# Decode attention on one core: engines without a closing barrier, PV of block 0 inside the PE loop, K of two blocks loaded first, and the last rows stored by two queues

## The chip, the cores and the metric

The kernel runs on one core of one Trainium2 chip. The metric is the device time of one execution in microseconds (us). Each DMA leaves 16 completion records in a trace (1776 for the 111 DMAs of the kernel before), and I count it landed at the last of them. A ratio is the mean time of one kernel's fast runs over that of the other kernel's fast runs of the same rounds, so it is not quite the ratio of the medians that stand beside it.

## The reference

```
q: [8, 16, 16, 256]   k, v: [8, 16, 2048, 256]   (bf16)
scores = einsum('bhqd,bhkd->bhqk', q, k) * 256 ** -0.5
attn   = softmax(scores, axis=-1)
out    = einsum('bhqk,bhkd->bhqd', attn, v)
```

There are 128 heads with 16 queries each. K and V are 134 MB each and every byte is used for 16 queries only, so the kernel is a way to stream 268 MB through the core.

## The kernel before

The profile names five engines: PE for the matrix products, DVE (here transposes, maxima and scaling), ACT (here exponentials, scaling and stores), POOL (nearly idle here) and SP (here the loads). `PEld` are PE's weight loads, and `SPq` or `ACTq` marks what the profile gives to an engine's sequencer, such as issuing a DMA. QK is the product that gives the scores, PV the one with V.

The heads are worked on in G = 16 blocks of 8. A block has two units (e = 0, 1) of 4 heads; a unit's K is 4 MB, and so is its V. `KN` holds two units of K and `VB` two units of V, so each load waits until its buffer is free: K until DVE has transposed the old K (`kt`), V of block g until PE has multiplied with V of block g-1 (`pv`).

For each block: DVE transposes K (8 instructions of 2.28 us), PE computes the scores (`qk`, 64 matmuls and 32 weight loads), DVE takes the maximum, ACT the exponential, DVE transposes the probabilities, PE multiplies with V (`pv`, 64 matmuls and 64 weight loads), ACT and DVE scale the result, and ACT stores it.

Every engine has its own list of jobs with semaphores between them. SP's list is the loads, in this order:

```python
        for u in (0, 1):
            k_load(u)                 # K of block 0, each unit in two halves
        v_load(0)
        k_load(2)                     # K of block 1, unit 0
        v_load(1)
        k_load(3)                     # K of block 1, unit 1, in two halves
        for g in range(2, G):
            for u in (2 * g, 2 * g + 1):
                k_load(u)
            for u in (2 * g - 2, 2 * g - 1):
                v_load(u)
        v_load(NU - 2)
        v_load(NU - 1)                # the last unit in pieces of 16 16 8 8 8 4 4 tiles
```

PE's list, of which the steady part is a loop (`nc.Fori`), so that its instructions stand in the program once:

```python
        qk_block(0)
        qk(1, 0, 0)
        qk(1, 0, 1)
        pv(0, 0)                      # PV of block 0 between the pieces of QK of block 1
        qk(1, 1, 0)
        qk(1, 1, 1)
        pv(0, 1)
        qk_block(2)
        for g in range(3, last):
            pv(g - 2, 0)
            pv(g - 2, 1)
            qk_block(g)
        # ... (cut: QK of the last block, PV of the last two)

        def emit_pe(eng):
            jobs = order["pe"]
            head, turns = jobs[:14], [jobs[14 + 6 * x:20 + 6 * x] for x in range(G - 4)]
            emit_jobs(eng, head)
            # ... (cut: checks that all turns wait alike)
            with nc.Fori(0, STEP * len(turns), STEP, ...) as it:
                # ... (cut: one turn, waiting for values that grow by STEP)
            emit_jobs(eng, jobs[14 + 6 * len(turns):])
```

The streams stand in a `Block`, which joins all engines in a barrier at its end. ACT stores the last rows and waits for them.

Of the kernel before, what the change touches and what calls it, by code (L numbers as in the profile page):

```python
# [12 lines left out]
HT = 32  # L13
# [12 lines left out]
def bass_standalone__softmax_full_bidir__sampling_kernel(  # L26
# [10 lines left out]
    G = NH // 8  # L37
    NU = 2 * G
    last = G - 1
# [4 lines left out]
    ku = k.rearrange("b h s d -> (b h s) d").rearrange("(u p t) d -> u p t d", p=128, t=NT)  # L44
# [3 lines left out]
    with ExitStack() as es:  # L48
        ec = es.enter_context
        KN = ec(nc.sbuf_tensor("KN", [128, 2, NT, D], BF16))  # L50
# [8 lines left out]
        O_fin = ec(nc.sbuf_tensor("O_fin", [128, 4, D], BF16))  # L59
# [11 lines left out]
        sem_kn = [ec(nc.semaphore("s_kn%d" % i)) for i in range(2)]  # L71
# [6 lines left out]
        def J(eng, cls, emit, deps=(), dma=None, inc=1):  # L78
            deps = [d for d in deps if d is not None]
            if dma is not None:  # L80
                jb = _Job(eng, cls, emit, deps, dma[0], dma[1], 16)
            else:
                if (eng, cls) not in counters:
                    counters[(eng, cls)] = [ec(nc.semaphore("c_%s_%s" % (eng, cls))), 0]
                c = counters[(eng, cls)]
                c[1] += inc
                jb = _Job(eng, cls, emit, deps, c[0], c[1], inc)
            order[eng].append(jb)
            return jb

        block = ec(nc.Block())

        QR = VB[:, 1, 0:SQ, :].rearrange("p s d -> p (s d)")
        KNf = KN[:].bitcast(F32)
        KBf = KB[:].bitcast(F32)
# [83 lines left out]
                ins = eng.matmul(O_ps[:, bank, 0:D], PT[:, t, :], buf[:, t, :], start=(t == 0), stop=(t == NT - 1))  # L179
            return ins  # L180

        def emit_store(eng, g, e=None):
            dst = out.rearrange("b h s d -> (b h s) d")[g * 128:(g + 1) * 128, :].rearrange("(e r) d -> e r d", e=2)
            if e is None:
                return eng.dma_start(dst.rearrange("e r d -> r e d"), O_fin[:, g % 2, :])
            return eng.dma_start(dst[e], O_fin[e:128:2, 2 + e, :])


        j_idz = J("pool", "prep", lambda eng: eng.memset(ident[:], 0.0))
# [9 lines left out]
        j_qwb, j_qt, j_exp, j_pt, j_px, j_max, j_rab = {}, {}, {}, {}, {}, {}, {}  # L199
        j_ea, j_eb, j_st = {}, {}, {}  # L200

        vparts = {NU - 2: [32, 32], NU - 4: [32, 32], NU - 1: [16, 16, 8, 8, 8, 4, 4]}

        def v_parts(u):
            return vparts.get(u, [HT, HT] if u % 2 else [NT])

        def k_load(u):

            g, e = u // 2, u % 2
            deps = [("kt", g - 1, e, 3)] if g else []  # L210
            if u in (0, 1, 3):
                for h in range(2):
                    j_k[u, h] = J("sp", "ld", lambda eng, h=h, n=HT: eng.dma_start(  # L213
                        KN[:, e, HT * h:HT * h + HT, :], ku[u, :, HT * h:HT * h + HT, :]), deps,
                        dma=(ec(nc.semaphore("s_k%d%d" % (u, h))), 16))
            else:
                n0 = len([x for x in range(e, u, 2) if x not in (0, 1, 3)])
                j_k[u, 0] = j_k[u, 1] = J("sp", "ld", lambda eng, n=NT: eng.dma_start(KN[:, e], ku[u]),
                                          deps, dma=(sem_kn[e], 16 * (n0 + 1)))

        def v_buf(u):

# [2 lines left out]
        def v_load(u):  # L225
            g, e = u // 2, u % 2
            j_v[u] = []
            a = 0
            for x, n in enumerate(v_parts(u)):
                deps = [("kt", g, e, 3)] if g == last else [("pv", g - 1, 1)] if g else [("qt", 0)] if e else []  # L230
                sem = (ec(nc.semaphore("s_vt%d_%d" % (u, x))), 16) if g >= last - 1 else (sem_v[e + x], 16 * (g + 1))
                j_v[u].append(J("sp", "ld", lambda eng, a=a, n=n: eng.dma_start(  # L232
                    v_buf(u)[:, a:a + n, :], vu[u, :, a:a + n, :]), deps, dma=sem))
                a += n


        for u in (0, 1):
            k_load(u)
        v_load(0)
        k_load(2)  # L240
        v_load(1)
        k_load(3)
        for g in range(2, G):
            for u in (2 * g, 2 * g + 1):
                k_load(u)
            for u in (2 * g - 2, 2 * g - 1):
                v_load(u)
        v_load(NU - 2)
        v_load(NU - 1)

# [11 lines left out]
        def qk(g, e, h):  # L262
            j_qk[g, e, h] = J("pe", "qk", lambda eng: emit_qk(eng, e, h),
                              [("kt", g, e, 2 * h + 1), ("qwb", g, e) if h == 0 else None,
                               ("exp", g - 1, h) if g and e == 0 else None])
# [7 lines left out]
        def pv(g, h):  # L273
            j_pv[g, h] = J("pe", "pv", lambda eng: emit_pv(eng, h),
                           [("px", g, h), ("eb", g - 1) if g and h == 0 else None]
                           + (j_v[2 * g] + j_v[2 * g + 1][:1] if h == 0 else j_v[2 * g + 1][1:]))
# [52 lines left out]
        def finish(e):  # L329

            j_eb[last, e] = J("dve", "eb", lambda eng: eng.tensor_scalar(  # L331
                out=O_fin[:, 2 + e, :], in0=O_ps[:, (2 * last + e + 1) % 4, 0:D], scalar1=rab[:, last, e:e + 1],
                scalar2=None, op0=ALU.mult), [("pv", last, 1, e), ("rab", last)])

        def finish_store(e):
            j_st[last, e] = J("act", "st", lambda eng: emit_store(eng, last, e), [("eb", last, e)],
                              dma=(ec(nc.semaphore("s_fin%d" % e)), 16))


        def qk_block(g):  # L340
            for e in range(2):
                for h in range(2):
                    qk(g, e, h)

        qk_block(0)
        qk(1, 0, 0)
        qk(1, 0, 1)
        pv(0, 0)
        qk(1, 1, 0)
        qk(1, 1, 1)  # L350
        pv(0, 1)
        qk_block(2)
        for g in range(3, last):
            pv(g - 2, 0)
            pv(g - 2, 1)
            qk_block(g)
# [19 lines left out]
            softmax_act(g)  # L376
        evac_a(last - 1)
        store(last - 1)
        finish_store(0)
        finish_store(1)  # L380

        j_qt[0] = J("dve", "qt", emit_qt, j_q)
        for g in range(G):
# [16 lines left out]
        px(last, 1)  # L400
        finish(0)
        finish(1)

        tables = {"kt": j_kt, "qwb": j_qwb, "qt": j_qt, "qk": j_qk, "exp": j_exp, "pt": j_pt, "px": j_px, "max": j_max,
                  "rab": j_rab, "ea": j_ea, "eb": j_eb, "st": j_st, "pv": j_pv}
# [12 lines left out]
        def emit_jobs(eng, jobs):  # L418
            known = {}
            for jb in jobs:  # L420
                for sem, val in needs(jb).values():
                    if known.get(id(sem), 0) < val:
                        eng.wait_ge(sem, val)
                        known[id(sem)] = val
                jb.emit(eng).then_inc(jb.sem, jb.inc)

        def emit_stream(eng, name):
            emit_jobs(eng, order[name])
            if name == "act":
                for key in (last - 2, last - 1, (last, 0), (last, 1)):  # L430
                    eng.wait_ge(j_st[key].sem, j_st[key].val)

        def emit_pe(eng):

            jobs = order["pe"]
            head, turns = jobs[:14], [jobs[14 + 6 * x:20 + 6 * x] for x in range(G - 4)]
            emit_jobs(eng, head)
            first = [needs(jb) for jb in turns[min(1, len(turns) - 1)]]
            base = 2 + min(1, len(turns) - 1)
            for x, turn in enumerate(turns):  # L440
                for n0, jb in zip(first, turn):
                    n1 = needs(jb)
                    assert all(key in n0 and n0[key][1] + STEP * (x + 2 - base) == val for key, (_, val) in n1.items())
            with nc.Fori(0, STEP * len(turns), STEP, engines=OrderedEngineSet([eng.engine]), head_slot={eng.engine: 0}) as it:
                offs = sorted({val - STEP * (base - 2) for n0 in first for _, val in n0.values()})
                at = {o: eng.snap(it + o) for o in offs}
                for jb, n0 in zip(turns[0], first):
                    for sem, val in n0.values():
                        eng.wait_ge(sem, at[val - STEP * (base - 2)])
                    jb.emit(eng).then_inc(jb.sem, jb.inc)  # L450
            emit_jobs(eng, jobs[14 + 6 * len(turns):])

        @block.sync
        def _(eng):
            emit_stream(eng, "sp")

        @block.tensor
        def _(eng):
            emit_pe(eng)

        @block.scalar
        def _(eng):
            emit_stream(eng, "act")

        @block.vector
        def _(eng):
            emit_stream(eng, "dve")

        @block.gpsimd
        def _(eng):  # L470
            emit_stream(eng, "pool")

# [1 line left out]
_INS = ['q', 'k', 'v']  # L474
_OUTS = [((8, 16, 16, 256), 'bfloat16')]
# [23 lines left out]
```

## Time and profile before

The median was 641.17 us.

| what | before |
|---|---|
| span | 639.5 us |
| bytes moved, mean rate over the span | 270.67 MB, 423 GB/s |
| first K load issued, last V load landed | 2.56 us, 636.05 us |
| landing to landing of 4 MB loads | 9.71 us (432 GB/s) |
| PE, DVE, ACT busy | 77%, 67%, 15% |

The page of the profile shows the 16 DMA engines busy from the first slice to the last (tenths of 40 slices of 16 us, and what they moved in each); among the DMA queues, q1 carries the loads, and q8 instruction packets, of 16 KB each (five, 0.08 MB; I take them for fetches of PE's program; the first came at 63.09 us):

```profile
DMA  9999999999999999999999999999999999999996
GB/s 319 436 427 427 438 419 440 428 427 434 426 434 426 430 441 424 443 426 429 428 426 437 428 430 437 421 446 416 441 428 426 435 424 437 435 427 435 421 422 253
...
q1 hardware_dynamic: 13152, 269.49, 98.7%
...
q8 instruction: 5, 0.08, 0.1%
...
DMA 72%; DVE 23%; PE 3%; issue 1%; SPq 0%; ACT 0%; DVEq 0%; ACTq 0%
```

The reader is to see that the loads are the bound: the chain that ended last is 72% DMA, and where it says DVE, a transpose only frees the buffer for a load that is queued behind others. So the rest of the work costs time only where it lets the load queue run dry.

The last V piece lands at 636.05 us, and the timeline (start, duration, engine, line, what) goes on:

```profile
636.75 0.48 DVE L331 TENSOR_SCALAR O_fin<-O_ps,rab 128x256 bf16<-128x256 f32 x1 [6.64 <-PE O_ps L179]
637.27 0.50 ACTq L186 DMA_DIRECT2D out_dram<-O_fin  x1
```

The store lands at 639.06 us, and a branch, a drain and the barrier of the block take until 639.55.

### The profile page before, as it was taken

To read this page: it belongs to the slowest core of one execution; us is meant where nothing else is said; L and a number is where in the kernel's file an instruction comes from. 1 tells how busy PE (TensorE), PEld (TensorE's weight loads), DVE (VectorE), ACT (ScalarE), POOL (GpSimd) and SP (SyncE) were. 2 spreads that over 40 slices of the span, in tenths; PEclk is the share of its full clock that TensorE was granted. 3 is DMA by queue.
4 is the path that set the end of the run, shared out by engine and by line. 5 is a ranking of instruction groups with operands and counts; after the bars stand their busy time and mean duration, and the time that the engine had idled before them with its cause. 6 is when DMAs were issued, how large, how long until landed. Compare 5 with 4: busy or idle time off the path is not lost.

```text
span 639.5 us, 4835 instructions
## 1 busy us (share of the span) xinstructions
PE 491.4 (77%) x2176; PEld 166.7 (26%) x1680; DVE 428.2 (67%) x372; ACT 99.1 (15%) x208; POOL 4.2 (1%) x7
## 2 busy tenths in 40 slices
PE   0827979876896768958688686797866878686998
PEld 0102313213131221412213132131311313122286
DVE  4866598693857938488483875939569395694861
ACT  2121203030120301202012120211203012030010
POOL 2000000000000000000000000000000000000000
PEclk9977989899897998979899798998989989799899
DMA  9999999999999999999999999999999999999996
GB/s 319 436 427 427 438 419 440 428 427 434 426 434 426 430 441 424 443 426 429 428 426 437 428 430 437 421 446 416 441 428 426 435 424 437 435 427 435 421 422 253
DMA packets 15483, 270.67 MB, mean 423 GB/s; under 512 B 1776, under 2 KB 3824, under 8 KB 4464
## 3 DMA queue, kind: packets, MB, share of 16 engines
q1 hardware_dynamic: 13152, 269.49, 98.7%
q10 hardware_dynamic: 2320, 1.05, 0.6%
q8 instruction: 5, 0.08, 0.1%
q14 instruction: 6, 0.05, 0.0%
HBM read 269.48 MB, written 1.05 MB: 423 GB/s over the span
## 4 chain that ended last, share of the span: by engine, by line
DMA 72%; DVE 23%; PE 3%; issue 1%; SPq 0%; ACT 0%; DVEq 0%; ACTq 0%
DMA KN<-in_k_dram 68%; DVE KB L128 22%; DMA KN<-in_v_dram 5%; PE O_ps L179 2%; PE S_ps L145 1%; PE S_ps L133 1%; DVE PC L159 0%; SPq L112 0%; DVE negm L150 0%; ACT QW L121 0%; DVE O_fin L331 0%; SPq L213 0%; SPq L232 0%; ACT P_sb L154 0%; DVE rab L300 0%
## 5 line engine op out<-in xcount | busy, mean ns | idle before, releaser
L128 DVE STREAM_TRANSPOSE KB<-KN 128x2048 f32<-128x2048 f32 x128 | 284.8, 2281 | 154.3 <-DMA KN<-in_k_dram 131.6
L145 PE MATMUL S_ps<-KB,QW 128*128 128x512 bf16 x528 | 215.9, 418 | 127.4 <-DVE KB L128 127.4
L173 PE MATMUL O_ps<-VB,PT 128*128 128x512 bf16 x896 | 198.9, 383 | 17.7 <-DMA VB<-in_v_dram 17.7
L133 PE MATMUL S_ps<-KB,QW 128*128 128x512 bf16 x496 | 207.1, 417 | 0.0
L145 PEld LDWEIGHTS S_ps<-KB,QW 128*128 128x128 bf16 x528 | 54.4, 103 | 333.8 <-issue 232.4
L173 PEld LDWEIGHTS O_ps<-VB,PT 128*128 128x128 bf16 x896 | 87.5, 99 | 131.8 <-issue 31.1
L121 ACT ACTIVATE QW<-QT 32x128 bf16<-32x128 bf16 x128 | 53.9, 421 | 334.4 <-PE S_ps L133 326.5
L165 DVE COPY PT<-PC 32x1024 bf16<-32x1024 bf16 x128 | 53.3, 416 | 4.3 <-PE O_ps L179 2.6
L159 DVE STREAM_TRANSPOSE PC<-P_sb 128x1024 bf16<-128x1024 bf16 x32 | 37.9, 1224 | 21.1 <-ACT P_sb L154 21.1
L150 DVE TENSOR_REDUCE negm<-S_ps 128x1 f32<-128x2048 f32 x16 | 36.7, 2292 | 7.9 <-PE S_ps L133 7.5
L154 ACT ACTIVATE P_sb<-S_ps,negm 128x1024 bf16<-128x1024 f32 x32 | 35.4, 1110 | 36.1 <-DVE negm L150 26.4
L316 ACT ACTIVATE O_tmp<-O_ps,rab 128x256 f32<-128x256 f32 x15 | 7.1, 474 | 144.2 <-PE O_ps L173 143.4
L179 PE MATMUL O_ps<-KN,PT 128*128 128x256 bf16 x128 | 14.4, 273 | 0.2 <-DMA KN<-in_v_dram 0.2
L179 PE MATMUL O_ps<-VB,PT 128*128 128x256 bf16 x128 | 14.1, 273 | 0.1
L179 PEld LDWEIGHTS O_ps<-VB,PT 128*128 128x128 bf16 x128 | 12.4, 98 | 2.0 <-DVE PT L165 0.6
L179 PEld LDWEIGHTS O_ps<-KN,PT 128*128 128x128 bf16 x128 | 12.3, 98 | 2.2 <-issue 0.5
L331 DVE TENSOR_SCALAR O_fin<-O_ps,rab 128x256 bf16<-128x256 f32 x2 | 1.0, 484 | 11.8 <-PE O_ps L179 11.8
L321 DVE SCALAR_TENSOR_TENSOR O_fin<-O_ps,rab,O_tmp 128x256 bf16<-128x256 f32 x15 | 6.7, 448 | 1.8 <-issue 1.8
L154 ACT ACTIVATION_READ_ACCUMULATOR P_sb<-S_ps,negm 128x1 f32 x32 | 6.3, 196 | 0.0
L115 DVE STREAM_TRANSPOSE QT<-VB 128x2048 f32<-128x2048 f32 x1 | 2.3, 2311 | 5.6 <-DMA VB<-in_q_dram 5.6
L300 DVE TENSOR_SCALAR rab<-mask,rinv 128x2 f32<-128x2 f32 x16 | 3.7, 229 | 0.6
L191 POOL MEMSET PT<- 128x4096 f32 x1 | 3.5, 3512 | 0.0
(11 smaller groups left out, 7.8 us busy)
## 6 DMA issues: line engine op xcount, KB each, us to landing
KN<-in_k_dram SPq DMA_DIRECT2D x29, 4096.0 KB, 29.8
VB<-in_v_dram SPq DMA_DIRECT2D x32, 2048.0 KB, 25.2
VB<-in_v_dram SPq DMA_DIRECT2D x14, 4096.0 KB, 20.0
KN<-in_k_dram SPq DMA_DIRECT2D x6, 2048.0 KB, 21.0
KN<-in_v_dram SPq DMA_DIRECT2D x2, 2048.0 KB, 27.7
KN<-in_v_dram SPq DMA_DIRECT2D x2, 1024.0 KB, 23.4
KN<-in_v_dram SPq DMA_DIRECT2D x3, 512.0 KB, 26.1
VB<-in_q_dram SPq DMA_DIRECT2D x4, 256.0 KB, 4.5
```

The source lines that it names most:

```text
L121: ins = eng.activation(ap_of(dv, dv.offset + 32 * a + e, [[256, 4], [128, 2], [2, 16]]), ap_of(sv, sv.offset + 2 * (2 * g + e), [[64, 4], ...
L128: return eng.transpose(KBf[:, c % R_KB].rearrange("p t i -> p (t i)"), KNf[:, e].rearrange("p t i -> p (t i)")[:, n * c:n * c + n])
L133: return eng.add_instruction(mybir.InstMatmult(start_tensor_calc=start, stop_tensor_calc=stop, ldweights=False, tile_size=(128, 128), tile ...
L145: ins = mm(S_ps[:, 2 * h + c, :], QW[:, e, bp, :], rhs, start=(e == 0 and bp == 0), stop=(e == 1 and bp == 7))
L150: return eng.tensor_reduce(out=negm[:, g:g + 1], in_=S_ps[:].rearrange("p c n -> p (c n)"), axis=AX.X, op=ALU.max, negate=True)
L154: return eng.activation(P_sb[:, 1024 * h:1024 * h + 1024], S_ps[:, 2 * h:2 * h + 2, :].rearrange("p c n -> p (c n)"), ACTF.Exp, bias=negm[ ...
L159: return eng.transpose(PC[:, h].rearrange("p t x -> p (t x)"), P_sb[:, 1024 * h:1024 * h + 1024])
L165: ins = eng.tensor_copy(PT[pr, 32 * h:32 * h + 32, pr], PC[pr, h])
L173: ins = eng.matmul(O_ps[:, 0, :], PT[:, t, :], rhs, start=(t == 0), stop=(t == NT - 1))
L179: ins = eng.matmul(O_ps[:, bank, 0:D], PT[:, t, :], buf[:, t, :], start=(t == 0), stop=(t == NT - 1))
L316: j_ea[g] = J("act", "ea", lambda eng: eng.activation(O_tmp[:], src, ACTF.Copy, scale=rab[:, g, 0:1]), [("pv", g, 1) if g < last - 1 else ...
L321: j_eb[g] = J("dve", "eb", lambda eng: eng.scalar_tensor_tensor(out=O_fin[:, g % 2, :], in0=src, scalar=rab[:, g, 1:2], in1=O_tmp[:], op0= ...
```

## The change

The intent: end each engine by itself, so that no barrier follows the last store; shorten PE's program by taking PV of block 0 into the loop, which then runs 13 turns and not 12; load K of blocks 0 and 1 before any V, in halves, so that QK of block 1 can be done before that PV; and halve the last store over two queues.

```diff
-        block = ec(nc.Block())
...
-        vparts = {..., NU - 1: [16, 16, 8, 8, 8, 4, 4]}
+        vparts = {..., NU - 1: [16, 16, 8, 8, 8, 4, 2, 2]}
...
-            if u in (0, 1, 3):
+            if g < 2:
                 for h in range(2):        # two halves; each now waits for its own half's transpose
...
-        for u in (0, 1):
-            k_load(u)
-        v_load(0)
-        k_load(2)
-        v_load(1)
-        k_load(3)
-        for g in range(2, G):
+        for g in range(G):
             for u in (2 * g, 2 * g + 1):
                 k_load(u)
-            for u in (2 * g - 2, 2 * g - 1):
-                v_load(u)
+            if g:
+                for u in (2 * g - 2, 2 * g - 1):
+                    v_load(u)
...
         qk_block(0)
-        qk(1, 0, 0)
-        qk(1, 0, 1)
-        pv(0, 0)
-        qk(1, 1, 0)
-        qk(1, 1, 1)
-        pv(0, 1)
-        qk_block(2)
-        for g in range(3, last):
+        qk_block(1)
+        for g in range(2, last):
             pv(g - 2, 0)
             pv(g - 2, 1)
             qk_block(g)
...
-        finish_store(0)
-        finish_store(1)
+        finish_store("act", 0, 0, 64)
...
+        finish_store("sp", 1, 0, 32)
+        finish_store("act", 1, 32, 64)
...
-            head, turns = jobs[:14], [jobs[14 + 6 * x:20 + 6 * x] for x in range(G - 4)]
+            head, turns = jobs[:8], [jobs[8 + 6 * x:14 + 6 * x] for x in range(G - 3)]
...
-        @block.sync
-        def _(eng):
-            emit_stream(eng, "sp")
...
+        emit_stream(nc.sync, "sp")
+        emit_stream(nc.scalar, "act")
+        emit_stream(nc.vector, "dve")
+        emit_stream(nc.gpsimd, "pool")
+        emit_pe(nc.tensor)
```

More of the change, by code (lines that the diff above doesn't have):

```diff
@@ L180, in emit_pv1, with emit_store @@
             return ins
-        def emit_store(eng, g, e=None):
+        def emit_store(eng, g, e=None, r0=0, r1=64):
             dst = out.rearrange("b h s d -> (b h s) d")[g * 128:(g + 1) * 128, :].rearrange("(e r) d -> e r d", e=2)
@@ L185, in emit_store @@
                 return eng.dma_start(dst.rearrange("e r d -> r e d"), O_fin[:, g % 2, :])
-            return eng.dma_start(dst[e], O_fin[e:128:2, 2 + e, :])
+            return eng.dma_start(dst[e, r0:r1], O_fin[2 * r0 + e:2 * r1:2, 2 + e, :])
         j_idz = J("pool", "prep", lambda eng: eng.memset(ident[:], 0.0))
@@ L200, in bass_standalone__softmax_full_bidir__sampling_kernel @@
         j_ea, j_eb, j_st = {}, {}, {}
-        vparts = {NU - 2: [32, 32], NU - 4: [32, 32], NU - 1: [16, 16, 8, 8, 8, 4, 4]}
+        vparts = {NU - 2: [32, 32], NU - 4: [32, 32], NU - 1: [16, 16, 8, 8, 8, 4, 2, 2]}
         def v_parts(u):
@@ L209, in k_load @@
             g, e = u // 2, u % 2
-            deps = [("kt", g - 1, e, 3)] if g else []
-            if u in (0, 1, 3):
+            if g < 2:
                 for h in range(2):
                     j_k[u, h] = J("sp", "ld", lambda eng, h=h, n=HT: eng.dma_start(
-                        KN[:, e, HT * h:HT * h + HT, :], ku[u, :, HT * h:HT * h + HT, :]), deps,
-                        dma=(ec(nc.semaphore("s_k%d%d" % (u, h))), 16))
+                        KN[:, e, HT * h:HT * h + HT, :], ku[u, :, HT * h:HT * h + HT, :]),
+                        [("kt", g - 1, e, 2 * h + 1)] if g else [], dma=(ec(nc.semaphore("s_k%d%d" % (u, h))), 16))
             else:
-                n0 = len([x for x in range(e, u, 2) if x not in (0, 1, 3)])
                 j_k[u, 0] = j_k[u, 1] = J("sp", "ld", lambda eng, n=NT: eng.dma_start(KN[:, e], ku[u]),
-                                          deps, dma=(sem_kn[e], 16 * (n0 + 1)))
+                                          [("kt", g - 1, e, 3)], dma=(sem_kn[e], 16 * (g - 1)))
         def v_buf(u):
@@ L333, in finish, with finish_store @@
                 scalar2=None, op0=ALU.mult), [("pv", last, 1, e), ("rab", last)])
-        def finish_store(e):
-            j_st[last, e] = J("act", "st", lambda eng: emit_store(eng, last, e), [("eb", last, e)],
-                              dma=(ec(nc.semaphore("s_fin%d" % e)), 16))
+        def finish_store(eng, e, r0, r1):
+            j_st[last, e, r0] = J(eng, "st", lambda eng: emit_store(eng, last, e, r0, r1),
+                                  [("eb", last, e)],
+                                  dma=(ec(nc.semaphore("s_fin%d_%d" % (e, r0))), 16))
         def qk_block(g):
@@ L428, in emit_stream @@
             emit_jobs(eng, order[name])
-            if name == "act":
-                for key in (last - 2, last - 1, (last, 0), (last, 1)):
-                    eng.wait_ge(j_st[key].sem, j_st[key].val)
+            for key in {"act": (last - 2, last - 1, (last, 0, 0), (last, 1, 32)), "sp": ((last, 1, 0),)}.get(name, ()):
+                eng.wait_ge(j_st[key].sem, j_st[key].val)
         def emit_pe(eng):
             jobs = order["pe"]
-            head, turns = jobs[:14], [jobs[14 + 6 * x:20 + 6 * x] for x in range(G - 4)]
+            head, turns = jobs[:8], [jobs[8 + 6 * x:14 + 6 * x] for x in range(G - 3)]
             emit_jobs(eng, head)
@@ L450, in emit_pe @@
                     jb.emit(eng).then_inc(jb.sem, jb.inc)
-            emit_jobs(eng, jobs[14 + 6 * len(turns):])
-        @block.sync
-        def _(eng):
-            emit_stream(eng, "sp")
-        @block.tensor
-        def _(eng):
-            emit_pe(eng)
-        @block.scalar
-        def _(eng):
-            emit_stream(eng, "act")
-        @block.vector
-        def _(eng):
-            emit_stream(eng, "dve")
-        @block.gpsimd
-        def _(eng):
-            emit_stream(eng, "pool")
+            emit_jobs(eng, jobs[8 + 6 * len(turns):])
+        emit_stream(nc.sync, "sp")
[3 more added lines that the diff above has]
+        emit_pe(nc.tensor)
 _INS = ['q', 'k', 'v']
```

## The prediction

> What bounds the kernel now: the K and V loads. The page's DMA row is 9 tenths in every slice but the last, 423 GB/s over the 639.5 us span; the chain of waits is 72% DMA. By the records of the SP queue's loads, 4 MB land every 9.71 us and the queue never runs dry, from the first K issue at 2.56 us to the last V landing at 636.05 us. Work moved in the middle can't show unless it starves that queue. What can: the head, the tail, disturbances of the stream.

> The tail before (timeline): last V lands 636.05; its 4 PV matmuls end 636.75; DVE's scaling ends 637.24; ACT issues the last store 637.27, landing 639.06; the barrier that closes the block runs from 639.1 to 639.55.

> What the change does:
> 1. No closing barrier, no branches: after the store's wait come 0.47 us of branch, drain and barrier, all critical. Saved: about 0.4 us.
> 2. Last V piece 2 tiles, not 4: two matmuls fewer after the landing, 2 x 0.108 = 0.2 us; one more DMA with shorter packets (a 2 KB packet took 84 ns, an eighth of a 16 KB one 77) costs about 0.1. Net 0.1.
> 3. Last store in halves on SP and ACT: issue to landing was 1.79 us, mostly latency: [...] Half the rows save perhaps 0.15 us.
> 4. K of blocks 0 and 1 first, in halves, then V0: the queue keeps a load ahead (K2's halves can go out at about 17 and 22 us, while K1 lands until 27; K3's at 28 and 32). No gain, no hole: at most +0.1 us.
> 5. PV of block 0 inside the loop: PE has slack (77% busy). PV(0) now ends at about 80 us by my estimate, so V of block 1 is issued some 5 us before the queue would drain. But the PE program gets shorter by some 220 instructions (96 of a QK block, 128 of a PV). [...] This trace shows five 16 KB instruction packets, 1.0 to 1.1 us each (63, 106, 576, 612, 625 us); the load landing after the first came 1.40 us late, never recovered; an 8 KB fetch at 486 us cost 0.98 us more. At the end DMA engines finish over about 3 us (DMA share 0.69 in 632 to 634 us), and the latest sets the last landing. 220 instructions are 14 KB: one PE fetch should go, likely an early one. Gain 0 to 1.4 us, depending on which DMA engine the others hit; I take 0.5; a loss of 0.5 is possible.

> Sum: 0.4 + 0.1 + 0.15 + 0.5, less 0.05: 1.1 us. Predicted 640.1 us, range 639.0 to 640.9. Faster by over 2% (under 628.3): 1%; within 2%: 98%; slower by over 2%: 1%.

> What would show it: nothing after the last store's waits; DVE's last scaling starting about 0.5 us after the last landing, not 0.7; the store's halves landing about 1.65 us after issue; four 16 KB instruction packets; the lateness at 67 us gone or moved; landings still 9.71 us apart.

> What would make it wrong: a hole in the load queue around 50 to 90 us; fetches falling on one DMA engine; the measured time, 1.7 us longer than the span, may hold a closing cost that grows when engines end apart.

"Mostly latency" in point 3 rests on the trace of before: the store's packets took 0.25 us (638.43 to 638.68) of the 1.79. The 0.15 us is my estimate; half of those 0.25 would be 0.13. The 14 KB of point 5 are 220 instructions of 64 bytes, a size that was not shown then; k_pool_stream, below, shows it for POOL (128 memsets to a packet of 8 KB).

## More of the kernel before

The granted clock is the share of PE's full clock that it was allowed.

The timeline between 60 and 93 us (start, duration, engine, line, what) shows PV of block 0 in its two halves, and SP issuing V of block 1 when the second is done; the table of stretches gives from and to in us, the length, the busy time of PE, its weight loads, DVE, ACT and POOL with instruction counts, the granted clock, the share of the DMA engines and GB/s:

```profile
60.70 7.07 PE L173 MATMUL O_ps<-VB,PT 128*128 128x512 bf16 x32
75.59 7.07 PE L173 MATMUL O_ps<-VB,PT 128*128 128x512 bf16 x32
82.69 1.28 SPq L232 DMA_DIRECT2D VB<-in_v_dram  x3
```

```profile
84.00:86.00 2.00, 0.00 (x0) 0.00 (x0) 2.00 (x2) 0.00 (x0) 0.00 (x0) 1.00 0.93 360
86.00:88.00 2.00, 1.26 (x4) 0.34 (x3) 2.00 (x2) 0.00 (x0) 0.00 (x0) 0.79 0.97 410
```

V of block 1 is issued at 82.69 us. The load ahead of it, K of block 2, lands at 86.97 us, 4.3 us later.

## The result, and the profile after

The changed kernel is slower: 646.05 us median (644.84 to 646.44, 6 runs), where the kernel before takes 641.19 us (640.97 to 641.36, 6 runs). The ratio is 1.0072 with a 95% interval of 1.0059 to 1.0085. That is within 2%, as forecast, but on the other side, and 5 us above the upper end of the range. The profiled run took 645.01 us with a span of 643.7 us. Its page, the lines that answer to those shown of before:

```profile
DMA  9999979999999999999999999999999999999996
GB/s 324 425 433 430 438 299 430 448 416 438 426 432 444 414 443 423 431 440 429 435 419 436 436 428 436 420 438 427 435 440 413 443 422 436 436 431 431 417 425 257
...
q1 hardware_dynamic: 13488, 269.51, 98.1%
...
q8 instruction: 5, 0.08, 0.1%
...
DMA 65%; DVE 23%; PE 10%; issue 1%; SPq 1%; ACT 0%; DVEq 0%; ACTq 0%
```

One slice, the sixth (80 to 97 us), fell from 419 to 299 GB/s: (419 - 299) x 16.1 us / 432 GB/s is 4.5 us of loading. PE has risen from 3% to 10% of the chain. And the fetches of instructions are still five. The stretches between 84 and 88 us:

```profile
84.00:86.00 2.00, 2.00 (x11) 0.87 (x9) 2.00 (x2) 0.00 (x0) 0.00 (x0) 1.00 0.16 66
86.00:88.00 2.00, 2.00 (x11) 0.78 (x8) 0.28 (x1) 0.25 (x1) 0.00 (x0) 1.00 0.00 0
```

The DMA engines come to a stand. The timeline says what they wait for:

```profile
72.12 15.60 PE L171 MATMUL O_ps<-VB,PT 128*128 128x512 bf16 x64 [3.39 <-issue]
...
87.75 1.28 SPq L229 DMA_DIRECT2D VB<-in_v_dram  x3
```

PV of block 0 ends at 87.72 us, and V of block 1 is issued at 87.75, not at 82.69. K of block 2 landed at 87.04 us, so the queue had run dry. By the records of the loads, V of block 1 then lands 13.57 us after the load ahead of it, where 4 MB need 9.71: 3.86 us are lost there, and they were not won back: the last V piece landed 4.43 us later than before.

Why is PV so late? QK of block 1 ends at 68.7 us, and PE then idles for 3.39 us though nothing of the program's is missing ("issue"). The record of PE's sequencer shows one instruction in that time: the compare-and-branch at the loop's entry, from 65.24 to 71.75 us, 6.50 us. In the kernel before the same branch took 0.30 us (at 101.27). One of the five 16 KB instruction packets falls in it, at 69.28 to 70.37 us. After the pause PE is slow as well; the stretches around it (the column before the last two is the granted clock):

```profile
68.70:72.10 3.40, 0.03 (x1) 0.01 (x1) 2.29 (x1) 2.63 (x5) 0.00 (x0) 0.99 1.08 458
72.10:75.40 3.30, 3.28 (x8) 1.15 (x9) 2.80 (x5) 1.34 (x4) 0.00 (x0) 0.50 1.06 452
75.40:88.00 12.60, 12.60 (x60) 5.54 (x57) 8.89 (x4) 0.25 (x1) 0.00 (x0) 1.00 0.70 302
```

The tail of the changed kernel, in the timeline:

```profile
641.14 0.48 DVE L323 TENSOR_SCALAR O_fin<-O_ps,rab 128x256 bf16<-128x256 f32 x1 [6.52 <-PE O_ps L177]
641.65 0.55 SPq L185 DMA_DIRECT2D out_dram<-O_fin  x1
641.65 0.52 ACTq L185 DMA_DIRECT2D out_dram<-O_fin  x1
```

The last V piece landed at 640.48 us, 4.43 us later than before; from there to the end of the span it is 3.23 us, where it was 3.50. So the end did win 0.27 us, and the loads lost 4.43.

### The profile page after: what moved, and what is told of

It reads as the page before. It is cut to its first block, busy times and chain, and to the rows that moved or that the text cites. A ratio compares the mean times of both kernels' runs of the same rounds, so it can differ in the third digit from the quotient of the medians.

```text
span 643.7 us, 4833 instructions
## 1 busy us (share of the span) xinstructions
PE 488.6 (76%) x2176; PEld 166.3 (26%) x1680; DVE 428.2 (67%) x372; ACT 99.1 (15%) x208; POOL 4.2 (1%) x7
## 4 chain that ended last, share of the span: by engine, by line
DMA 65%; DVE 23%; PE 10%; issue 1%; SPq 1%; ACT 0%; DVEq 0%; ACTq 0%
DMA KN<-in_k_dram 65%; DVE KB L126 21%; PE O_ps L177 4%; PE O_ps L171 2%; PE S_ps L143 2%; PE S_ps L131 1%; DVE PT L163 1%; DVE PC L157 0%; DVE negm L148 0%; SPq L110 0%; SPq L211 0%; ACT P_sb L152 0%; SPq L229 0%; DVE O_fin L323 0%; DVE O_fin L313 0%
```

## The experiments

**The theory** after reading the traces: the loop's entry, which now lies at about the 200th PE instruction (192 matmuls and weight loads and 8 waits and the like), not at about the 430th, makes PE's sequencer wait for its next instructions; the pause and the slow clock after it hold PV of block 0 back by 5 us; and that is more than the load queue had to spare. **The first rival**: PV of block 0 behind QK of block 1 is too late by its order, wherever it stands. **The second**: the new order of the loads, which puts V of block 0 last, makes the hole.

### a_peel: the same order, the loop one turn later

```diff
-            head, turns = jobs[:8], [jobs[8 + 6 * x:14 + 6 * x] for x in range(G - 3)]
+            head, turns = jobs[:14], [jobs[14 + 6 * x:20 + 6 * x] for x in range(G - 4)]
```

> The changed kernel with its first loop turn (PV of block 0 and QK of block 2) written out ahead of the loop; order of all work as in the changed kernel. Theory 1 (loop entry: the branch of 6.5 us at 65 us and the slow matmuls after it held PV of block 0 back, so V of block 1 was issued at 87.75 us, after the queue had run dry at about 86): the branch no longer stands before PV of block 0, V of block 1 is issued at 82 to 84 us, the 3.9 us hole before the landing at 100.6 us goes, time 640 to 641 us. Rival (PV of block 0 behind QK of block 1 is too late by its order alone): V still issued at 86 us or later, time 643 us or more.

Measured: 640.77 us (640.58 to 641.12, 4 runs), before 641.23 in the same rounds; ratio 0.9992 (0.9976 to 1.0007). The timeline, then the stretches:

```profile
68.08 13.97 PE L171 MATMUL O_ps<-VB,PT 128*128 128x512 bf16 x64
82.08 1.28 SPq L229 DMA_DIRECT2D VB<-in_v_dram  x3
```

```profile
84.00:86.00 2.00, 1.63 (x8) 0.24 (x3) 2.00 (x2) 0.00 (x0) 0.00 (x0) 1.00 0.77 328
86.00:88.00 2.00, 1.63 (x8) 0.48 (x5) 1.18 (x2) 0.00 (x0) 0.00 (x0) 1.00 1.10 475
```

PE goes from QK to PV without a pause, V of block 1 goes out at 82.08 us, 5.67 us earlier and 5.0 us before K of block 2 lands (87.11), and the hole is gone. Order of work and of loads are those of the changed kernel, so both rivals fall for it. In this run too a 16 KB instruction packet came at 69.32 us, at the same place in PE's work; in straight code it held nobody up (PV took 13.97 us without a gap). So the fetch by itself did not stop PE here; the pause came where the entry branch met it, 6.50 us around the packet at 69.28.

### b_pv_in_loop and g_old_loads_peeled: the old order of loads

In b_pv_in_loop only PE's order and the loop of the change are put into the kernel before (the lines of the diff from `qk_block(1)` and of `head, turns`). In g_old_loads_peeled the order is the same, but that turn is written out ahead of the loop (its edit against the kernel before):

```diff
-        qk(1, 0, 0)
-        qk(1, 0, 1)
+        qk_block(1)
         pv(0, 0)
-        qk(1, 1, 0)
-        qk(1, 1, 1)
         pv(0, 1)
         qk_block(2)
         for g in range(3, last):
```

> The kernel before with only PV of block 0 moved into the loop. Theory: with the old load order K of block 1 lands last at 67.5 us, QK of block 1 ends at about 76 us and PV of block 0 only starts then, ending about 90 us without and 94 us with a slow loop entry; K of block 2 has landed by 87 us, so the hole is 5 to 9 us and the time 646 to 650 us. Rival (the new load order makes the hole): no hole, 641 us.

> The kernel before (block, old load order, one store) with PV of block 0 behind QK of block 1, but written out ahead of the loop. Theory: with the old load order this order is too late by itself: the entry stall of 3.2 us of PE time goes, V of block 1 is issued at about 89 us, after the queue has run dry at 87, hole about 5 to 6 us, time 646 to 648 us. Rival (the slow loop entry alone made the 8.7 us hole): V issued before 86 us, no hole, 641.2 us.

Measured: b_pv_in_loop 650.30 us (650.16 to 650.45, 4 runs; ratio 1.0138), with the entry branch at 70.85 us taking 6.87 us, V of block 1 issued at 92.09 us and 8.67 us lost at its landing. g_old_loads_peeled 646.84 us (646.17 to 647.96, 4 runs; ratio 1.0094), with V of block 1 issued at 88.11 us; its timeline and stretches:

```profile
74.10 13.97 PE L173 MATMUL O_ps<-VB,PT 128*128 128x512 bf16 x64
88.11 1.28 SPq L232 DMA_DIRECT2D VB<-in_v_dram  x3
```

```profile
84.00:86.00 2.00, 2.00 (x11) 0.91 (x10) 2.00 (x2) 0.00 (x0) 0.00 (x0) 1.00 0.04 16
86.00:88.00 2.00, 2.00 (x11) 0.84 (x9) 2.00 (x2) 0.00 (x0) 0.00 (x0) 1.00 0.00 0
```

So with the old loads the order alone is too late: K of block 1 lands at 67 us and not at 47, QK of block 1 ends at 74 us, and a hole of 4.6 us opens at V's landing without any pause of PE. The entry adds 4.0 us to it (88.11 to 92.09). The new order of loads is what makes PV behind QK possible at all; it just doesn't leave enough for the pause.

### c_pv_undone: the new order of loads with the old order of PE

The change with `qk(1, 0, ...), pv(0, 0), qk(1, 1, ...), pv(0, 1), qk_block(2)` back ahead of the loop.

> The changed kernel with PV of block 0 back between the QK pieces of block 1, ahead of the loop; new load order, no closing barrier and the split store kept. Theory 1: V of block 1 issued before 82 us, no hole, 640 to 640.5 us. Rival (the load order is to blame: V of block 0 lands 10 us later): a hole remains, 642 us or more.

Measured: 640.86 us (640.66 to 641.55, 4 runs; ratio 0.9994, 0.9979 to 1.0009). V of block 1 is issued at 82.45 us and there is no hole (DMA share 0.72 and 1.14 in the two stretches); issue and time are each some 0.4 us over what was expected. The load order costs nothing, and gains nothing either: d_tail_only, below, has the old one and takes 640.69.

### e_pad64 and e_pad32: the same loop, entered later in the program

The changed kernel with needless weight loads in QK of the first blocks: a matmul that reused the weights of the one ahead loads them again. 64 of them in blocks 0 and 1, or 32 in block 0; the results are the same.

```diff
-                    mm = eng.matmul if c == cs[0] else (lambda *x, **y: mm_kept(eng, *x, **y))
+                    mm = eng.matmul if c == cs[0] or again else (lambda *x, **y: mm_kept(eng, *x, **y))
...
-            ... lambda eng: emit_qk(eng, e, h),
+            ... lambda eng: emit_qk(eng, e, h, again=g < 2),     # e_pad32: g < 1
```

> The changed kernel with 64 needless weight loads added to QK of blocks 0 and 1 (results unchanged), so that the loop is entered at about the 264th PE instruction, not the 200th. Theory 1a (the branch waits because the next 16 KB of PE instructions, from the 256th on, have not arrived when it is reached): an earlier fetch, in straight code, has brought them; the entry branch takes 0.2 to 0.4 us, V of block 1 is issued at 82 to 84 us, 640.5 to 641.2 us. Rival (any loop entry so early in the run is slow, wherever it lies in the program): branch 6 to 7 us, 644 us or more.

> The same with 32 needless weight loads, in QK of block 0 alone: the loop is entered at about the 232nd PE instruction, still in the first 256. Theory 1a with a boundary at 256: still slow, branch 5 to 7 us, 644 to 646 us. If it is fast (0.2 to 0.4 us, about 640.8 us), the boundary lies between 200 and 232 and is not that of the 16 KB block counted from the program's start.

Measured: e_pad64 640.72 us (640.48 to 641.48, 4 runs), e_pad32 640.69 us (640.46 to 640.97, 4 runs), both with the entry branch taking 0.31 us, at 64.85 and 65.87 us, just when the changed kernel's took 6.50. The timeline and stretches of e_pad32:

```profile
69.17 13.97 PE L171 MATMUL O_ps<-VB,PT 128*128 128x512 bf16 x64
83.18 1.28 SPq L229 DMA_DIRECT2D VB<-in_v_dram  x3
```

```profile
84.00:86.00 2.00, 2.00 (x11) 0.48 (x5) 2.00 (x1) 0.00 (x0) 0.00 (x0) 1.00 0.74 279
86.00:88.00 2.00, 2.00 (x11) 0.41 (x5) 1.17 (x2) 0.00 (x0) 0.00 (x0) 1.00 1.18 508
```

This is the sharpest test: added work, and 5 us less. The rival "an entry so early in the run is slow" falls, and what counted is the place in the program (the 232nd instruction at 65.87 us against the 200th at 65.24). But my boundary was wrong: at the 232nd instruction, still in the first 256, the entry is quick. (256 was my estimate: a packet of 16 KB at 64 bytes an instruction, a size that k_pool_stream shows for POOL, counted from the program's start. No trace shows where in the program a packet begins.) What the traces show is when the 16 KB packets came:

```
                entry branch        16 KB instruction packets around it
after           65.24, 6.50 us      69.28 and 75.17 us    (none earlier)
b_pv_in_loop    70.85, 6.87 us      75.24 and 81.13       (none earlier)
e_pad32         65.87, 0.31 us      58.68, then 70.31
e_pad64         64.85, 0.31 us      58.81, then 68.99
before         101.27, 0.30 us      63.09, then 105.79
a_peel          96.23, 0.31 us      69.32, then 100.19
```

Where the first 16 KB packet of the run had come before the entry, the entry was quick; where it had not, it waited until 1.4 us after that packet's end. In all six a packet comes 4.0 to 4.5 us after the branch began. What exactly the branch waits for is inferred from these times; the limit lies between the 200th and the 232nd instruction, and I did not narrow it.

### d_tail_only, i_no_block, h_one_store and f_best: the end of the kernel

d_tail_only is the kernel before with all three changes to the end; i_no_block with the block alone taken away; h_one_store is d_tail_only with the last store whole on ACT; f_best is h_one_store with smaller pieces of V earlier:

```diff
-        finish_store("sp", 1, 0, 32)
-        finish_store("act", 1, 32, 64)
+        finish_store("act", 1, 0, 64)          # h_one_store and f_best
-        NU - 1: [16, 16, 8, 8, 8, 4, 2, 2]
+        NU - 1: [16, 16, 8, 8, 4, 4, 4, 2, 2]  # f_best
```

> The kernel before with only the changes to the end: no block and closing barrier, last V piece in 2 and 2 tiles, last store in two halves on two queues. Predicted for these three: 0.4 + 0.1 + 0.15, so about 640.5 us. Rival (nothing gained, since the store latency and the close outside the span take it back): 641.2 us.

> The kernel before with the block and its closing barrier taken away, nothing else. Theory: the 0.47 us from the last store's wait to the end of the barrier goes: 640.7 to 640.8 us. Rival (the close moves outside the span): 641.2 us.

> d_tail_only with the last store whole on ACT again, so no block and last V pieces of 2 and 2 tiles only. Theory: store 1.79 us from issue to landing, not 2.02, and no second close: 640.45 us, 0.2 us under d_tail_only. Rival (two queues save issue time): above d_tail_only's 640.69 us.

> The kernel before without block and closing barrier, last V pieces 8, 8, 4, 4, 4, 2, 2 (last of all), last store whole on ACT. From the traces: the half on SP landed 2.02 us after issue, the whole one on ACT 1.79, so 0.23 us less than with two queues; PE no longer arrives late at the last piece (in the runs so far its last 16 matmul steps of 0.109 us ran without a gap behind the third piece of 8): 0.1 to 0.2 us less. Expected 640.3 us (640.0 to 640.6); rival (the tail does not set the time): 640.7 us.

| kernel | median (5 runs, range) | before, same rounds | last V landing to DVE's scaling | store, issue to landing | store's landing to end of span |
|---|---|---|---|---|---|
| before | | 641.2 | 0.70 us | 1.79 us | 0.49 us |
| i_no_block | 640.46 (640.22 to 640.68) | 641.20 | 0.70 | 1.78 | 0.06 |
| d_tail_only | 640.69 (640.35 to 641.13) | 641.23 | 0.68 | 2.02 (SP), 1.76 (ACT) | 0.03 |
| h_one_store | 640.33 (640.18 to 640.65) | 641.20 | 0.67 | 1.75 | 0.06 |
| f_best | 640.26 (640.13 to 640.55) | 641.18 | 0.48 | 1.76 | 0.06 |

The last three columns are from one trace of each. Every ratio's interval reaches up to about 1 (0.9973 to 1.0000 for h_one_store, 0.9974 to 1.0001 for f_best), so by that measure the gain is not clear; still, all 5 runs of i_no_block, h_one_store and f_best lie below all runs of before in their rounds.

The barrier's going is most of the gain: 0.43 us of the span by the traces. The time outside the span fell too: i_no_block's 5 runs take 1.42 to 1.48 us more than their spans, the 9 runs of before in its rounds 1.74 to 1.82, and in all the experiments no run without the block is above 1.53 and none with it below 1.73. That is another 0.33 us, and with it the sum is about the 0.74 us by which the medians differ. Halving the store loses: the DMA issues of d_tail_only (issuing queue, KB, us to landing) against those of f_best, the stretch after 636.5 us:

```profile
out_dram<-O_fin SPq DMA_DIRECT2D x1, 16.0 KB, 2.0
out_dram<-O_fin ACTq DMA_DIRECT2D x1, 16.0 KB, 1.8
```

```profile
out_dram<-O_fin ACTq DMA_DIRECT2D x1, 32.0 KB, 1.8
```

ACT's 16 KB land no sooner than its 32 KB did, and SP's 16 KB 0.26 us later than ACT's, so SP is now the last to end. The time on ACT did not grow with the size here (1.76 us for 16 KB, 1.75 to 1.79 for 32), and SP's half, issued at the same moment (636.99 us), lost 0.26 us, so the second queue saved nothing. (The halves are different rows as well, and no run swaps them.)

The last V piece of 2 tiles and not 4 gained 0.03 us, for PE wasn't waiting for it: from the landing of the third piece of 8 on, its last 16 matmul steps of 0.109 us run without a gap, and end as late whatever the pieces are. f_best breaks up that piece of 8, and the 0.70 us become 0.48.

f_best is the fastest kernel that I ran: 640.26 us, 0.9 us under the kernel before in its rounds, and 5.8 under the changed one's median of other rounds.

### k_pool_stream: are fetches of instructions hidden?

The prediction made much of the fetches, so this prices them. f_best with 1536 memsets of one column on POOL, which is idle; nobody waits for them, but they are 96 KB of instructions (by the twelve packets of 8 KB below).

```diff
+        def emit_junk(eng):
+            for x in range(1536):
+                ins = eng.memset(junk[:, x:x + 1], 0.0)
+            return ins
+        J("pool", "junk", emit_junk)
```

> f_best with 1536 one-column memsets added on the idle POOL engine, in straight code after its preparations: nothing waits for them, but POOL's program grows by 96 KB, which its sequencer must fetch while the loads run. Theory (fetches take time on the DMA engines that carry the loads, and the latest engine sets the end): more instruction packets, landings late by 0.3 to 1.5 us where one hits the latest engine, time 641 to 643 us. Rival (fetches are hidden): 640.26 us, as f_best.

Measured: 651.34 us (650.74 to 651.74, 4 runs), ratio 1.0157, far above the 641 to 643 us expected. Twelve 8 KB packets more were fetched, one per 128 memsets and about one per 5 us until 68 us, and with each the load landing behind it was about 0.66 us late: 2 MB landed every 5.55 us and not every 4.89. All those delays add up (7.7 us by 69 us), though the DMA engines together moved almost as much (421 GB/s against 431 from 10 to 66 us). The memsets' own writes didn't slow the loads' packets: 16 KB took 0.61 us (the median) in both kernels. The stretch from 10 to 30 us of k_pool_stream, then of f_best:

```profile
10.00:30.00 20.00, 10.39 (x39) 2.13 (x20) 14.05 (x7) 4.94 (x12) 16.83 (x506) 1.00 1.01 430
```

```profile
10.00:30.00 20.00, 11.70 (x44) 2.45 (x23) 16.17 (x9) 5.06 (x12) 0.00 (x0) 1.00 1.03 437
```

430 GB/s and 437 can't explain landings that come 13% further apart. A load has landed at the last of its 16 completion records, and in the kernel before these lie 0.62 to 0.65 us apart for every K or V load that landed up to 61.28 us, and 1.99 us in the load behind the fetch at 63.09 us. The reading that fits is that one engine of the 16, hit by every fetch of POOL's stream, fell behind while the others ran ahead. I infer it from the sum; the records don't name the engine. The other 3 us of the 11 are a hole of 2.65 us at V of block 1 (DVE's transposes came later too) and smaller delays. So these fetches were not free, about 0.66 us each, and the size of an idle engine's program counted.

## Why the prediction was wrong

The sign was wrong. Point by point:

1. *"No closing barrier ... Saved: about 0.4 us."* Right for the span: 0.49 us became 0.03 in the changed kernel's, 0.43 us less in i_no_block's. It left out the 0.33 us that went outside the span.
2. *"Last V piece 2 tiles, not 4 ... Net 0.1."* Too large: 0.03 us. It took the two matmuls for time that PE waits through after the last landing; but PE was working back to back there, and the end of its run was set by the landing of an earlier piece of 8.
3. *"Half the rows save perhaps 0.15 us."* Wrong in sign: the halves took 2.02 and 1.78 us where the whole took 1.79; the latency hardly depended on the rows, as the prediction itself said ("mostly latency"), and SP's half was slower than ACT's.
4. *"K of blocks 0 and 1 first ... No gain, no hole."* Right for the load order by itself: c_pv_undone 640.86 against d_tail_only 640.69.
5. *"PV(0) now ends at about 80 us by my estimate, so V of block 1 is issued some 5 us before the queue would drain."* **This is the step that failed.** PV ended at 87.72 us. The estimate left out: 2 us because QK of block 1 began at half clock after an idle time of 14.5 us (granted clock 0.50 from 49.9 to 55.0 us); 3.4 us of PE idle at the loop's entry; 1.6 us because PV then began at half clock too (0.50 for 3.3 us). The first alone would have done no harm: a_peel has it, issues V at 82.08 us and shows no hole. The entry of the loop added the other 5.0 us, and 3.86 us of loading were lost. The room was smaller than predicted too. Take from V's issue what was lost at its landing: in the changed kernel, b_pv_in_loop and g_old_loads_peeled that leaves 83.9, 83.4 and 83.5 us, so any issue later than that costs time, although K of block 2 lands only at about 87; e_pad32's, at 83.18, cost nothing. The prediction's 80 us and 5 us to spare put that limit at 85. The prediction looked at the same fetches and asked only what they cost the DMA engines, not what a branch that meets one costs PE (6.50 us for the entry branch here, 3.39 of them idle).
6. *"One PE fetch should go."* Wrong: five before, five after, though PE's program is some 220 instructions shorter. In each of the six traces tabled above, wherever the loop begins, a packet comes 4.0 to 4.5 us after its entry branch began.

The list of what would make it wrong began with *"a hole in the load queue around 50 to 90 us"*, and that is what came, at 86 us; I had given it too little weight for a margin of 5 us built from estimates.

Two things stay open. The changed kernel's runs fall near 645 us (three from 644.84 to 645.79) and near 646.4 us (three); the trace is of one at 645.01, and what adds 1.4 us to the others wasn't looked into. And after the hole the fetch at 295 us delayed a landing by 1.02 us, where before the change it was 0.31; why, no run tests.

## What to carry to other kernels

When a buffer's release moves later, compute the margin of the queue that it feeds from the trace, with the clock that PE has after each idle time (0.50 for 3.3 us after 3.39 us idle here, for 5.0 us after 14.5); count it to some 3 us before the load ahead lands (83.4 to 83.9 against 87 us here), not to the landing; and treat a margin of a few microseconds as none unless it was measured. Look at the entry of a loop: where no 16 KB instruction packet had come before it, the entry branch took 6.50 and 6.87 us here, and 0.30 to 0.31 where one had, so write the first turn out ahead of the loop when a tight buffer hangs on it. In this kernel, which the loads bind, a fetch of instructions delayed the load behind it (by about 0.66 us for 8 KB of POOL's in k_pool_stream, by 1.40 for PE's first 16 KB in the kernel before), and what reads as "shorter program" has to be checked by counting the instruction packets.
